# A decoder block at one token on one core: activations become the stationary matmul operand, weights and values stream 512 columns at a time

## The chip, the cores and the metric

The kernel runs on one core of a Trainium2 chip. The metric is the time of the program on the device in microseconds (us), the median of several runs. PE is TensorE (matmuls; PEld is its weight load), DVE is VectorE, ACT is ScalarE, POOL is GpSimd, and SP is SyncE, whose queue issues the big loads.

## What is computed

Eight sequences (B = 8) decode one token each through one block with D = 1024. The reference, cut to what matters:

```python
mod = (silu(c) @ w_mod).reshape(8, 6, 1, -1)            # sa, ca, ga, sb, cb, gb
h = layernorm(x) * (1 + ca) + sa
q = h @ wq                                              # 32 heads of 128
scores = q . k_cache * 128 ** -0.5                      # 4 kv heads, 8192 keys each
o = softmax(scores) @ v_cache
x = x + ga * (o @ wo)
h = layernorm(x) * (1 + cb) + sb
gate, up = h @ W_gate, h @ W_up                         # F = 3584
x = x + gb * ((gate * (gate > 0) * up) @ W_down)
```

All inputs are bf16. Eight query heads share one kv head, so there are 32 pairs (kv head, sequence), numbered n, each with 2 MB of k and 2 MB of v. With the weights 185.6 MB come from HBM, each byte once.

## The kernel before

**Recording and waits.** The program is written once, in order, through helpers (`mm`, `tr`, `dve`, `act`, `pool`). A small graph keeps each engine's instructions in that order and adds semaphore waits where one engine uses what another wrote. A PSUM bank (2 KB a partition, 8 banks) counts as one object: PE and another engine that touch the same bank wait for each other. Since all work passes through the helpers, most rows of the profile carry the helpers' lines: L278 is `mm`, L282 `tr`, L286 `dve`, L289 `act`, L510 the loads.

**Loads.** One ring of 11 x 8192 columns in SBUF takes all weights, k and v in a fixed order (`stream`): four blocks of `w_mod`, four of `wq`, then k(n) and, two pairs later, v(n), with a `wo` block for each kv head among them, then `gate` and `up` alternating, then `wd` (W_down). SP issues one DMA for each block in that order. A block that reuses ring space first waits for PE's last use of the blocks that lay there (`behind`, `users`).

**Matmuls with the weights stationary.** For mod, wq, wo, gate and up, a 128x128 piece of the weight is loaded into PE as the stationary operand, and the activations (128x8) move. The results lie transposed, output features on partitions, which is the form the next stage needs. Only `wd` works the other way: `hmT` (128x8) is stationary, 256 columns of weight move, and each of four matmuls writes another group of output partitions (0, 32, 64, 96).

**Attention.** The loop over n has eight slots j, each for 1024 keys. For a slot the kernel transposes eight 128x128 pieces of k on PE (`slot_transpose`), evicts them from PSUM (`slot_evac`: even slots DVE, odd slots ACT), multiplies the slot of two before with q (`slot_scores`, 8 matmuls), and does the values of pair n-2 (`slot_pv`, 8 matmuls with v stationary and `pt`, the exponentials, moving). Softmax of pair n-1 is spread over slots 2 to 7: `soft_max` (DVE maximum, `mp`), `soft_max_t` (transpose on PE), `soft_diag` (DVE: `nm`, then the diagonal `dg`), `soft_bc` (an f32 matmul that spreads the maximum), `soft_sub` (DVE, `ssub`), `soft_exp` (ACT, `pt`), `soft_sum` (eight matmuls with ones). `o_evac` divides by the sum at slot 0 of pair n+3. `wo_part` and `wo_add` follow every eight pairs.

**End.** After attention come the second layernorm, gate/up, relu and product (`hmT`), `wd`, and four small stores.

Of the kernel before, what the change touches and what calls it, by code (L numbers as in the profile page):

```python
# [124 lines left out]
def bass_adaLN_cond__gqa_block_cached__glu_gated_reglu__decode_kernel(  # L125
# [35 lines left out]
    with ExitStack() as es:  # L161
# [13 lines left out]
        onesb = sb("onesb", [128, 128], bf16)  # L175
# [5 lines left out]
        yacc = sb("yacc", [128, KD * B], f32)  # L181
# [13 lines left out]
        rl = sb("rl", [128, REP], f32)  # L195
        ot = sb("ot", [128, G, REP, B], bf16)
        gr = sb("gr", [128, KF * B], f32)
# [4 lines left out]
        crow, xrow, sig = (KT[0:B, i, :] for i in range(3))  # L202
        fR = ssub[:, 0:256]
# [9 lines left out]
        O = lambda i: PS[:, 5 + i, :]  # L213
        X = PS[:, 7, :]
        pS = [("ps", 0), ("ps", 1)]
        pT = [("ps", 2), ("ps", 3), ("ps", 4)]
        pO = [("ps", 5), ("ps", 6)]
        pX = ("ps", 7)
        g.psum(*pS, *pT, *pO, pX)
# [24 lines left out]
        wd_parts = [(0, 7), (7, 14), (14, 21), (21, 26), (26, 28)]  # L244
        for i, (a, z) in enumerate(wd_parts):
            block(("wd", i), (z - a) * D, B_W_down.rearrange("(p k) n -> p k n", k=KF)[:, a:z, :], (z - a, D))
# [51 lines left out]
        for t, v, k in ((identb, 0.0, "identb"), (identf, 0.0, "identf"), (onesD, 1.0 / D, "onesD"), (ones1, 1.0, "ones1"), (onesb, 1.0, "onesb")):  # L298
            pool(lambda e, t=t, v=v: e.memset(t[:], v), writes=[k])
        for t, k in ((identb, "identb"), (identf, "identf")):  # L300
            pool(lambda e, t=t: e.affine_select(out=t[:], in_=t[:], compare_op=ALU.not_equal, fill=1.0, base=0,
                                                pattern=[[-1, 128]], channel_multiplier=1), reads=[k], writes=[k])

# [7 lines left out]
        for k in range(KD):  # L311
            tr(TB(0)[:, B * k:B * (k + 1)], sig[:, k::KD], identb[0:B, 0:B], [("KT", 2), "identb"], [pT[0]])
        dve("tensor_copy", siluT[:], TB(0)[:, 0:KD * B].rearrange("p (k b) -> p k b", b=B), reads=[pT[0]], writes=["siluT"])
# [23 lines left out]
        NM = 6 * KD  # L337
        for k in range(KD):
            w = place[("mod", k // 2)][:, k % 2, :]
            for f in range(NM):  # L340
                mm(S(0)[:, B * f:B * (f + 1)], w[:, 128 * f:128 * (f + 1)], siluT[:, k, :], k == 0 and f == 0, k == KD - 1,
                   ["siluT"], [pS[0]], ("mod", k // 2))
        dve("tensor_copy", modT[:].rearrange("p s k b -> p (s k b)"), S(0)[:, 0:NM * B], reads=[pS[0]], writes=["modT"])
# [5 lines left out]
        for k in range(KD):  # L349
            w = place[("wq", k // 2)][:, k % 2, :]  # L350
            for h in range(Hq):
                mm(S(1)[:, B * h:B * (h + 1)], w[:, 128 * h:128 * (h + 1)], hT[:, k, :], k == 0 and h == 0, k == KD - 1,
                   ["hT"], [pS[1]], ("wq", k // 2))
        act(qT[:], S(1)[:, 0:Hq * B].rearrange("p (h b) -> p b h", b=B), ACT.Copy, reads=[pS[1]], writes=["qT"])
# [33 lines left out]
        def slot_pv(n, j):  # L388
            o = O(n % 2)[:, 0:REP]
            for i in range(8):  # L390
                cc = 8 * j + i
                mm(o, place[("v", n)][:, cc, :], pt[:, n % 2, REP * cc:REP * (cc + 1)], cc == 0, cc == NC - 1,
                   [("pt", n % 2)], [pO[n % 2]], ("v", n))
# [21 lines left out]

        def soft_sum(n):
            for i in range(8):
                mm(O(n % 2)[:, 64:128], onesb[:], pt[:, n % 2, 64 * i:64 * (i + 1)], i == 0, i == 7, ["onesb", ("pt", n % 2)], [pO[n % 2]])

        def o_evac(n):  # L420
            gg, b = n // B, n % B
            dve("tensor_reduce", lsum[:], O(n % 2)[:, 64:128].rearrange("p (c r) -> p r c", r=REP), AX.X, ALU.add, reads=[pO[n % 2]], writes=["lsum"])
            dve("reciprocal", rl[:], lsum[:], reads=["lsum"], writes=["rl"])
            dve("tensor_tensor", out=ot[:, gg, :, b], in0=O(n % 2)[:, 0:REP], in1=rl[:], op=ALU.mult, reads=[pO[n % 2], "rl"], writes=[("ot", gg)])

        def wo_part(gg, bank, h0, h1):
            w = place[("wo", gg)]
            for h in range(h0, h1):
                for k in range(KD):
                    mm(O(bank)[:, 128 + B * k:128 + B * (k + 1)], w[:, h, 128 * k:128 * (k + 1)], ot[:, gg, h, :], h == 0 and k == 0, h == REP - 1,  # L430
                       [("ot", gg)], [pO[bank]], ("wo", gg))

        def wo_add(gg, bank):
            y = O(bank)[:, 128:128 + KD * B]
            if gg == 0:
                dve("tensor_copy", yacc[:], y, reads=[pO[bank]], writes=["yacc"])
            else:
                dve("tensor_tensor", out=yacc[:], in0=y, in1=yacc[:], op=ALU.add, reads=[pO[bank], "yacc"], writes=["yacc"])

        for n in range(N + 4):  # L440
# [3 lines left out]
            wbank = (n - 1) % 2  # L444
            for j in range(8):
# [5 lines left out]
                if 0 <= n - 2 < N:  # L451
                    slot_pv(n - 2, j)
                if j == 0 and 0 <= n - 3 < N:
                    o_evac(n - 3)
                if wg is not None and 2 <= j <= 5:
                    wo_part(wg, wbank, 2 * (j - 2), 2 * (j - 1))
                if wg is not None and j == 6:
                    wo_add(wg, wbank)
# [95 lines left out]
```

## Time and profile before

| | |
|---|---|
| median of 3 runs | 452.18 us (452.06 to 452.18) |
| profiled execution, its own time | 452.11 us |
| its span, first to last instruction | 450.3 us |
| mean granted PE clock | 0.799 |
| PE, DVE, ACT busy | 357.0, 175.2, 155.1 us |
| read from HBM | 185.63 MB, 412 GB/s over the span |

An entry of the profile such as `L278 PE MATMUL PS<-qT,KT` reads line, engine, operation, output from inputs; `128x8 bf16 x2048` are partitions by elements, type and count. A matmul's time in a row is its passage through the pipeline; successive matmuls overlap, so the cost of a group is read from start to start in the timeline. A matmul with f32 operands appears as two. "Granted clock" is the share of PE's full clock that the throttle let through; 0.50 and 1.0 are the values recorded. "DMA share" is the mean busy share of the core's 16 DMA engines.

### The profile page before, as it was taken

To read this page: it belongs to the slowest core of one execution; us is meant where nothing else is said; L and a number is where in the kernel's file an instruction comes from. 1 tells how busy PE (TensorE), PEld (TensorE's weight loads), DVE (VectorE), ACT (ScalarE), POOL (GpSimd) and SP (SyncE) were. 2 spreads that over 40 slices of the span, in tenths; PEclk is the share of its full clock that TensorE was granted. 3 is DMA by queue.
4 is the path that set the end of the run, shared out by engine and by line. 5 is a ranking of instruction groups with operands and counts; after the bars stand their busy time and mean duration, and the time that the engine had idled before them with its cause. 6 is when DMAs were issued, how large, how long until landed. Compare 5 with 4: busy or idle time off the path is not lost.

```text
span 450.3 us, 16982 instructions
## 1 busy us (share of the span) xinstructions
PE 357.0 (79%) x8008; PEld 342.8 (76%) x8008; DVE 175.2 (39%) x422; ACT 155.1 (34%) x169; POOL 1.5 (0%) x11
## 2 busy tenths in 40 slices
PE   1525477887898959998989798898999999759973
PEld 1425377887888959888888798888889988649961
DVE  1001044554454434555544436445454446530000
ACT  3000055455444433444454335444453455400000
POOL 1000000000000000000000000000000000000000
PEclk9999998899796775888886859669787689955555
DMA  8999999999999999999999999999999999999992
GB/s 352 421 426 427 437 424 431 426 426 428 427 429 425 414 436 426 432 424 429 425 418 430 426 427 429 425 427 426 417 428 429 428 429 418 385 424 425 430 385 115
DMA packets 18101, 186.73 MB, mean 415 GB/s; under 512 B 1472, under 2 KB 1504, under 8 KB 7792
## 3 DMA queue, kind: packets, MB, share of 16 engines
q1 hardware_dynamic: 17968, 185.61, 97.6%
q8 instruction: 62, 1.02, 0.8%
q14 instruction: 7, 0.06, 0.0%
q10 hardware_dynamic: 64, 0.04, 0.0%
HBM read 185.63 MB, written 0.02 MB: 412 GB/s over the span
## 4 chain that ended last, share of the span: by engine, by line
DMA 49%; PE 35%; DVE 8%; SPq 4%; issue 3%; ACT 0%; DVEq 0%
DMA ring<-in_A_k_cache_dram 34%; PE PS L282 20%; PE PS L278 15%; DMA ring<-in_A_wq_dram 8%; DMA ring<-in_B_W_down_dram 7%; SPq L510 4%; DVE KT L286 3%; DVE mp L286 2%; DVE dg L286 1%; DVE nm L286 1%; DVE ssub L286 0%; ACT KT L289 0%; ACT pt L289 0%; DVE x1T L286 0%; DVE outR L286 0%
## 5 line engine op out<-in xcount | busy, mean ns | idle before, releaser
L282 PE MATMUL PS<-identb,ring 128*128 128x128 bf16 x2048 | 191.6, 249 | 10.9 <-DMA ring<-in_A_k_cache_dram 10.2
L289 ACT ACTIVATE KT<-PS 128x1024 bf16<-128x1024 bf16 x128 | 131.1, 1024 | 185.2 <-PE PS L282 142.9
L282 PEld LDWEIGHTS PS<-identb,ring 128*128 128x128 bf16 x2048 | 147.1, 112 | 13.7 <-DMA ring<-in_A_k_cache_dram 11.6
L286 DVE COPY KT<-PS 128x1024 bf16<-128x1024 bf16 x128 | 88.5, 692 | 149.1 <-PE PS L282 149.1
L278 PE MATMUL PS<-qT,KT 128*128 128x8 bf16 x2048 | 92.7, 169 | 0.1
L278 PE MATMUL PS<-pt,ring 128*128 128x8 bf16 x2048 | 87.3, 167 | 0.7 <-issue 0.7
L278 PEld LDWEIGHTS PS<-qT,KT 128*128 128x128 bf16 x2048 | 87.0, 102 | 0.2 <-ACT KT L289 0.2
L278 PEld LDWEIGHTS PS<-pt,ring 128*128 128x128 bf16 x2048 | 70.6, 98 | 1.0 <-issue 1.0
L278 PE MATMUL PS<-dg,ones 8*128 8x8 f32 x64 | 13.3, 278 | 25.5 <-DVE dg L286 25.5
L278 PEld LDWEIGHTS PS<-dg,ones 8*128 8x128 f32 x64 | 10.6, 204 | 28.2 <-DVE dg L286 27.8
L278 PEld LDWEIGHTS PS<-h2T,ring 128*128 128x128 bf16 x448 | 28.5, 172 | 2.0 <-DMA ring<-in_B_W_up_dram 1.6
L278 PE MATMUL PS<-h2T,ring 128*128 128x8 bf16 x448 | 28.7, 204 | 1.5 <-DMA ring<-in_B_W_up_dram 1.5
L286 DVE TENSOR_TENSOR ssub<-PS,nb 128x512 f32<-128x512 f32 x32 | 22.1, 692 | 1.2
L278 PE MATMUL PS<-siluT,ring 128*128 128x8 bf16 x384 | 10.9, 168 | 14.0 <-DMA ring<-in_w_mod_dram 14.0
L286 DVE TENSOR_REDUCE mp<-PS 128x8 f32<-128x512 f32 x32 | 21.8, 681 | 0.4 <-PE PS L278 0.4
L278 PEld LDWEIGHTS PS<-siluT,ring 128*128 128x128 bf16 x384 | 10.8, 105 | 14.3 <-DMA ring<-in_w_mod_dram 14.3
L289 ACT ACTIVATE pt<-ssub 128x512 bf16<-128x512 f32 x32 | 19.9, 622 | 3.7 <-DVE ssub L286 3.7
L278 PE MATMUL PS<-pt,onesb 128*128 128x64 bf16 x256 | 15.7, 215 | 2.6 <-ACT pt L289 2.6
L278 PE MATMUL PS<-hT,ring 128*128 128x8 bf16 x256 | 7.5, 168 | 11.2 <-DMA ring<-in_A_wq_dram 11.2
L278 PEld LDWEIGHTS PS<-hT,ring 128*128 128x128 bf16 x256 | 7.1, 104 | 11.5 <-DMA ring<-in_A_wq_dram 11.5
L289 ACT ACTIVATE qT<-PS 128x256 bf16<-128x256 f32 x1 | 0.4, 384 | 42.7 <-PE PS L278 42.7
L278 PEld LDWEIGHTS PS<-pt,onesb 128*128 128x128 bf16 x256 | 11.9, 111 | 2.8 <-ACT pt L289 2.8
(64 smaller groups left out, 107.1 us busy)
## 6 DMA issues: line engine op xcount, KB each, us to landing
ring<-in_A_k_cache_dram SPq DMA_DIRECT2D x32, 2048.0 KB, 38.3
ring<-in_A_v_cache_dram SPq DMA_DIRECT2D x32, 2048.0 KB, 37.6
ring<-in_w_mod_dram SPq DMA_DIRECT2D x4, 3072.0 KB, 20.7
ring<-in_A_wq_dram SPq DMA_DIRECT2D x4, 2048.0 KB, 42.3
ring<-in_A_wo_dram SPq DMA_DIRECT2D x4, 2048.0 KB, 43.0
ring<-in_B_W_gate_dram SPq DMA_DIRECT2D x4, 1792.0 KB, 27.9
ring<-in_B_W_up_dram SPq DMA_DIRECT2D x4, 1792.0 KB, 26.5
ring<-in_B_W_down_dram SPq DMA_DIRECT2D x3, 1792.0 KB, 28.8
```

Of the source, the lines that this page charges most:

```text
L278: return pe(lambda e: e.matmul(out_, lhsT, rhs, start=start, stop=stop, skip_group_check=True), reads, writes, block, deps)
L282: return pe(lambda e: e.matmul(out_, in_, ident, start=True, stop=True, is_transpose=True), reads, writes, block)
L286: return g.op("dve", lambda e: getattr(e, name)(*args, **kw), reads, writes)
L289: return g.op("act", lambda e: e.activation(*args, **kw), reads, writes)
L510: o.fn = (lambda e, key=key, src=src, o=o: e.dma_start(place[key], src).then_inc(o.sem, 16))
```

## The change

Every matmul with weights or values is turned round, as `wd` was before.

- **mod, wq, wo, gate, up:** the activations (128x8) are stationary and 512 columns of weight move; four successive matmuls write four groups of output partitions (0, 32, 64, 96) of one PSUM bank. The results come out in rows, one sequence a partition, so they are evicted whole and transposed back on PE: 12 f32 transposes for mod, 8 bf16 for q, 8 bf16 for `hmT`. The banks are zeroed first by DVE memsets, since the partitions between the groups are not written. The wo results add up in rows (`yR`), and four f32 matmuls with the selector `pick` turn them at the end.
- **PV:** 32 columns of `pt` (4 key pieces x 8 heads) are stationary and 512 columns of v move, 16 matmuls a pair in slots 1, 3, 5 and 7. Of the result V, four diagonal blocks are wanted. ACT copies the bank (`pv_evac`, slot 0 of pair n+3), four f32 matmuls with the selector `sel` add the blocks into Y (`pv_pick`, slot 1), and `o_evac` is in slot 2.
- **Sum:** a DVE reduction over `pt` (`soft_part`, slot 6) and one f32 matmul with ones (`soft_sum`, slot 7) replace the eight matmuls.
- **Softmax pieces:** `soft_max` moves from slot 2 to 1 and its transpose from 3 to 2; `soft_diag` is in slot 3, `soft_bc` and `soft_sub` in 4, `soft_exp` in 5. Each PE piece now stands one slot after the DVE piece that feeds it.
- **`wd` loads:** another split of the rows of W_down, with 8 KB and 4 KB runs per partition instead of 14, 10 and 4 KB. All other loads, their order and their ring places stay.

The diff, cut:

```diff
...
+        wd_parts = [(0, 2, 0, 4), (2, 4, 0, 4), (4, 6, 0, 4), (6, 7, 0, 2), (6, 7, 2, 4)]
+        for i, (a, z, i0, i1) in enumerate(wd_parts):
+            block(("wd", i), (z - a) * (i1 - i0) * D, B_W_down.rearrange("(c p i) n -> p c (i n)", p=128, i=4)[:, a:z, D * i0:D * i1],
+                  (z - a, (i1 - i0) * D))
...
+        dve("tensor_reduce", sel[:], identf[:].rearrange("p (q x) -> p x q", q=4), AX.X, ALU.add, reads=["identf"], writes=["sel"])
+        dve("tensor_reduce", pick[:], identf[:].rearrange("p (s h x) -> p h x s", s=2, h=2)[:, :, 0:B, :], AX.X, ALU.add, reads=["identf"], writes=["pick"])
+        for bank, key in ((S(0), pS[0]), (S(1), pS[1]), (T(0), pT[0]), (Y, pY)):
+            dve("memset", bank, 0.0, writes=[key])
...
-        NM = 6 * KD
+        mbank = [(S(0), pS[0]), (S(1), pS[1]), (T(0), pT[0])]
         for k in range(KD):
             w = place[("mod", k // 2)][:, k % 2, :]
-            for f in range(NM):
-                mm(S(0)[:, B * f:B * (f + 1)], w[:, 128 * f:128 * (f + 1)], siluT[:, k, :], k == 0 and f == 0, k == KD - 1,
-                   ["siluT"], [pS[0]], ("mod", k // 2))
-        dve("tensor_copy", modT[:].rearrange("p s k b -> p (s k b)"), S(0)[:, 0:NM * B], reads=[pS[0]], writes=["modT"])
+            for f in range(12):
+                j, q = f // 4, f % 4
+                mm(mbank[j][0][32 * q:32 * q + B, :], siluT[:, k, :], w[:, 512 * f:512 * (f + 1)], k == 0, k == KD - 1,
+                   ["siluT"], [mbank[j][1]], ("mod", k // 2))
+        for j in range(3):
+            if j == 1:
+                act(modR[j], mbank[j][0], ACT.Copy, reads=[mbank[j][1]], writes=[("KT", j)])
+            else:
+                dve("tensor_copy", modR[j], mbank[j][0], reads=[mbank[j][1]], writes=[("KT", j)])
+        tbank = [(T(1), pT[1]), (T(2), pT[2]), (V, pV)]
+        for j in range(3):
+            t, key = tbank[j]
+            for i in range(4):
+                tr(t[:, 128 * i:128 * (i + 1)], modR[j][:, 128 * i:128 * (i + 1)], identf[:], [("KT", j), "identf"], [key])
+            dve("tensor_copy", modT[:].rearrange("p s k b -> p (s k) b")[:, 16 * j:16 * (j + 1), :].rearrange("p (q i) b -> p i q b", i=4),
+                t.rearrange("p (i q x) -> p i q x", i=4, q=4)[:, :, :, 0:B], reads=[key], writes=["modT"])
...
-            for h in range(Hq):
-                mm(S(1)[:, B * h:B * (h + 1)], w[:, 128 * h:128 * (h + 1)], hT[:, k, :], k == 0 and h == 0, k == KD - 1,
-                   ["hT"], [pS[1]], ("wq", k // 2))
-        act(qT[:], S(1)[:, 0:Hq * B].rearrange("p (h b) -> p b h", b=B), ACT.Copy, reads=[pS[1]], writes=["qT"])
+            for f in range(8):
+                j, q = f // 4, f % 4
+                mm(S(j)[32 * q:32 * q + B, :], hT[:, k, :], w[:, 512 * f:512 * (f + 1)], k == 0, k == KD - 1,
+                   ["hT"], [pS[j]], ("wq", k // 2))
...
-        def slot_pv(n, j):
-            o = O(n % 2)[:, 0:REP]
-            for i in range(8):
-                cc = 8 * j + i
-                mm(o, place[("v", n)][:, cc, :], pt[:, n % 2, REP * cc:REP * (cc + 1)], cc == 0, cc == NC - 1,
-                   [("pt", n % 2)], [pO[n % 2]], ("v", n))
+
+        def pv(n, t):
+            for q in range(4):
+                cc = 16 * t + 4 * q
+                mm(V[32 * q:32 * (q + 1), :], pt[:, n % 2, REP * cc:REP * (cc + 4)],
+                   place[("v", n)][:, cc:cc + 4, :].rearrange("p c d -> p (c d)"), t == 0, t == 3, [("pt", n % 2)], [pV], ("v", n))
+
+        def pv_evac(n):
+            act(ov[:], V, ACT.Copy, reads=[pV], writes=["ov"])
+
+        def pv_pick(n):
+            for i in range(4):
+                mm(Y[:, 0:REP], ov[:, 128 * i:128 * (i + 1)], sel[:, REP * i:REP * (i + 1)], i == 0, i == 3, ["ov", "sel"], [pY])
...
+        def soft_part(n):
+            dve("tensor_reduce", lsum[:], pt[:, n % 2, :].rearrange("p (c r) -> p r c", r=REP), AX.X, ALU.add, reads=[("pt", n % 2)], writes=["lsum"])
+
         def soft_sum(n):
-            for i in range(8):
-                mm(O(n % 2)[:, 64:128], onesb[:], pt[:, n % 2, 64 * i:64 * (i + 1)], i == 0, i == 7, ["onesb", ("pt", n % 2)], [pO[n % 2]])
+            mm(X[:, 136:136 + REP], onesf[:], lsum[:], True, True, ["onesf", "lsum"], [pX])
+            dve("reciprocal", rl[:, n % 2, :], X[:, 136:136 + REP], reads=[pX], writes=[("rl", n % 2)])
 
         def o_evac(n):
             gg, b = n // B, n % B
-            dve("tensor_reduce", lsum[:], O(n % 2)[:, 64:128].rearrange("p (c r) -> p r c", r=REP), AX.X, ALU.add, reads=[pO[n % 2]], writes=["lsum"])
-            dve("reciprocal", rl[:], lsum[:], reads=["lsum"], writes=["rl"])
-            dve("tensor_tensor", out=ot[:, gg, :, b], in0=O(n % 2)[:, 0:REP], in1=rl[:], op=ALU.mult, reads=[pO[n % 2], "rl"], writes=[("ot", gg)])
-
-        def wo_part(gg, bank, h0, h1):
+            dve("tensor_tensor", out=ot[:, gg, :, b], in0=Y[:, 0:REP], in1=rl[:, n % 2, :], op=ALU.mult, reads=[pY, ("rl", n % 2)], writes=[("ot", gg)])
+
+
+        def wo_part(gg, h0, h1):
             w = place[("wo", gg)]
             for h in range(h0, h1):
-                for k in range(KD):
-                    mm(O(bank)[:, 128 + B * k:128 + B * (k + 1)], w[:, h, 128 * k:128 * (k + 1)], ot[:, gg, h, :], h == 0 and k == 0, h == REP - 1,
-                       [("ot", gg)], [pO[bank]], ("wo", gg))
-
-        def wo_add(gg, bank):
-            y = O(bank)[:, 128:128 + KD * B]
+                for half in range(2):
+                    a = 64 * (h % 2) + 32 * half
+                    mm(Y[a:a + B, :], ot[:, gg, h, :], w[:, h, 512 * half:512 * (half + 1)], h < 2, h >= REP - 2, [("ot", gg)], [pY], ("wo", gg))
+
+        def wo_add(gg):
             if gg == 0:
-                dve("tensor_copy", yacc[:], y, reads=[pO[bank]], writes=["yacc"])
+                dve("tensor_copy", yR[:], Y, reads=[pY], writes=["yR"])
             else:
-                dve("tensor_tensor", out=yacc[:], in0=y, in1=yacc[:], op=ALU.add, reads=[pO[bank], "yacc"], writes=["yacc"])
+                dve("tensor_tensor", out=yR[:], in0=Y, in1=yR[:], op=ALU.add, reads=[pY, "yR"], writes=["yR"])
 
         for n in range(N + 4):
             wg = (n - 11) // B if n >= 11 and (n - 11) % B == 0 else None
             if n == N + 3:
                 wg = G - 1
-            wbank = (n - 1) % 2
             for j in range(8):
                 if n < N:
                     slot_transpose(n, j)
                     slot_evac(n, j)
                 if 0 <= 8 * n + j - 2 < 8 * N:
                     slot_scores(8 * n + j - 2)
-                if 0 <= n - 2 < N:
-                    slot_pv(n - 2, j)
-                if j == 0 and 0 <= n - 3 < N:
-                    o_evac(n - 3)
-                if wg is not None and 2 <= j <= 5:
-                    wo_part(wg, wbank, 2 * (j - 2), 2 * (j - 1))
+                if 0 <= n - 3 < N:
+                    if j == 0:
+                        pv_evac(n - 3)
+                    elif j == 1:
+                        pv_pick(n - 3)
+                    elif j == 2:
+                        o_evac(n - 3)
+                if 0 <= n - 2 < N and j % 2 == 1:
+                    pv(n - 2, j // 2)
+                if wg is not None and 3 <= j <= 6:
+                    wo_part(wg, 2 * (j - 3), 2 * (j - 2))
                 if wg is not None and j == 6:
-                    wo_add(wg, wbank)
+                    wo_add(wg)
                 if 0 <= n - 1 < N:
-                    if j == 2:
+                    if j == 1:
                         soft_max(n - 1)
+                    elif j == 2:
+                        soft_max_t(n - 1)
                     elif j == 3:
-                        soft_max_t(n - 1)
+                        soft_diag(n - 1)
                     elif j == 4:
-                        soft_diag(n - 1)
                         soft_bc(n - 1)
+                        soft_sub(n - 1)
                     elif j == 5:
-                        soft_sub(n - 1)
+                        soft_exp(n - 1)
                     elif j == 6:
-                        soft_exp(n - 1)
+                        soft_part(n - 1)
                     elif j == 7:
                         soft_sum(n - 1)
...
-        dve("tensor_tensor", out=x1T[:].rearrange("p k b -> p (k b)"), in0=yacc[:], in1=modT[:, 2].rearrange("p k b -> p (k b)"), op=ALU.mult, reads=["yacc", "modT"], writes=["x1T"])
+        for i in range(4):
+            mm(X[:, 16 * i:16 * (i + 1)], yR[:, 128 * i:128 * (i + 1)], pick[:].rearrange("p h b -> p (h b)"), True, True, ["yR", "pick"], [pX])
+        dve("tensor_tensor", out=x1T[:].rearrange("p (h i) b -> p h i b", h=2), in0=X[:, 0:64].rearrange("p (i h b) -> p h i b", i=4, h=2),
+            in1=modT[:, 2].rearrange("p (h i) b -> p h i b", h=2), op=ALU.mult, reads=[pX, "modT"], writes=["x1T"])
...
+        for j in range(2):
+            dve("memset", S(j), 0.0, writes=[pS[j]])
+            dve("memset", T(j), 0.0, writes=[pT[j]])
+        dve("memset", V, 0.0, writes=[pV])
         for k in range(KD):
-            for half, nm_ in ((0, "gate"), (1, "up")):
+            for bank, keys, nm_ in ((S, pS, "gate"), (T, pT, "up")):
                 w = place[(nm_, k // 2)][:, k % 2, :]
-                for f in range(KF):
-                    mm(S(half)[:, B * f:B * (f + 1)], w[:, f::KF], h2T[:, k, :], k == 0 and f == 0, k == KD - 1,
-                       ["h2T"], [pS[half]], (nm_, k // 2))
-        act(gr[:], S(0)[:, 0:KF * B], ACT.Relu, reads=[pS[0]], writes=["gr"])
-        dve("memset", PS[:, 2, 0:256], 0.0, writes=[pT[0]])
-        dve("tensor_tensor", out=hmT[:].rearrange("p k b -> p (k b)"), in0=S(1)[:, 0:KF * B], in1=gr[:], op=ALU.mult, reads=[pS[1], "gr"], writes=["hmT"])
-
-
-        for i, (a, z) in enumerate(wd_parts):
-            for k in range(a, z):
-                for q in range(4):
-                    mm(PS[32 * q:32 * q + B, 2, 0:256], hmT[:, k, :], place[("wd", i)][:, k - a, 256 * q:256 * (q + 1)], k == 0, k == KF - 1,
-                       ["hmT"], [pT[0]], ("wd", i))
-        dve("tensor_tensor", out=fR, in0=PS[:, 2, 0:256], in1=gbR[:], op=ALU.mult, reads=[pT[0], "gbR"], writes=["ssub"])
+                for f in range(7):
+                    j, q = f // 4, f % 4
+                    mm(bank(j)[32 * q:32 * q + B, :], h2T[:, k, :], w[:, 512 * f:512 * (f + 1)], k == 0, k == KD - 1,
+                       ["h2T"], [keys[j]], (nm_, k // 2))
+        for j in range(2):
+            act(gr[j], S(j), ACT.Relu, reads=[pS[j]], writes=[("KT", j)])
+            dve("tensor_tensor", out=hmR[:, 512 * j:512 * (j + 1)], in0=T(j), in1=gr[j], op=ALU.mult, reads=[pT[j], ("KT", j)], writes=[("KT", 2 + j)])
+
+        for j in range(2):
+            for i in range(4):
+                tr(TB(2)[:, 512 * j + 128 * i:512 * j + 128 * (i + 1)], hmR[:, 512 * j + i:512 * (j + 1):4], identb[:], [("KT", 2 + j), "identb"], [pT[2]])
+        for j in range(2):
+            nq = 4 - j
+            dve("tensor_copy", hmT[:, 16 * j:16 * j + 4 * nq, :].rearrange("p (q i) b -> p i q b", i=4),
+                TB(2)[:, 512 * j:512 * (j + 1)].rearrange("p (i q x) -> p i q x", i=4, q=4)[:, :, 0:nq, 0:B], reads=[pT[2]], writes=["hmT"])
+
+
+        for n, (a, z, i0, i1) in enumerate(wd_parts):
+            for c_ in range(a, z):
+                for i in range(i0, i1):
+                    for q in range(4):
+                        at = D * (i - i0) + 256 * q
+                        mm(V[32 * q:32 * q + B, 0:256], hmT[:, 4 * c_ + i, :], place[("wd", n)][:, c_ - a, at:at + 256], c_ + i == 0, c_ == 6 and i == 3,
+                           ["hmT"], [pV], ("wd", n))
...
```

## The prediction

> **What bounds the kernel now.** I read the page first, then the stages, then the waits, then single instructions.
>
> ```profile
> PE 357.0 (79%) x8008; PEld 342.8 (76%) x8008; DVE 175.2 (39%) x422; ACT 155.1 (34%) x169; POOL 1.5 (0%) x11
> ...
> DMA  8999999999999999999999999999999999999992
> ...
> q1 hardware_dynamic: 17968, 185.61, 97.6%
> q8 instruction: 62, 1.02, 0.8%
> ```
>
> TensorE (PE) is busiest of the compute engines, but the DMA engines stand at 9 from slice 2 to 39, and q1 fills 97.6% of 16 engines' span. The chain of waits (DMA 49%, PE 35%) misleads about PE: during PE's pieces of it the loads ran on.
>
> The stages show what the last slice hides (last columns: granted clock, DMA share, GB/s):
>
> ```profile
> 60.00:390.00 330.00, 289.75 (x6564) 282.29 (x6562) 162.26 (x376) 148.36 (x160) 0.00 (x0) 0.81 1.01 425
> 400.00:430.00 30.00, 25.59 (x393) 24.76 (x393) 2.92 (x12) 0.21 (x1) 0.00 (x0) 0.50 1.02 427
> 437.00:445.00 8.00, 3.45 (x60) 1.60 (x56) 0.00 (x0) 0.00 (x0) 0.00 (x0) 0.50 0.49 204
> 446.40:450.30 3.90, 0.57 (x8) 0.08 (x8) 0.85 (x2) 0.00 (x0) 0.00 (x0) 0.50 0.02 4
> ```
>
> From 437 to 445 us half of the DMA capacity idles while PE waits for `wd` blocks: some engines are done and others are not. The trace keeps the 16 increments by which each load reports. Their spread, first to last, is 0.74 us for the first load, 1.7 at the load landing at 33.6, and 10.1 at 349.4. It grows in steps, at the landings of 88.6, 138.6, 198.6, 244.1, 299.0, 349.4 and 399.1: seven steps of 1.2 to 1.4 us, 1.3 on average. The packets of q8, PE's instruction fetch (16,384 B each), number 62 from 18.0 to 439.1 us; their durations repeat with period eight (934, 933, 924, 968, 960, 949, 886, 886 ns), so I read them as dealt in turn to eight engines. Packets 9, 17, 25, 33, 41, 49 and 57 start at 86.1, 136.1, 192.5, 241.8, 293.5, 345.7 and 394.8: each step belongs to one packet of the first of these engines. That engine carries 8 packets. The last load's first increment comes at 437.0 and its last at 446.33; then 3.97 us of matmuls, two DVE operations and stores end the span. So the bound is the slowest DMA engine: its share of the loads plus eight fetches.
>
> PE has little room in attention:
>
> ```profile
> PE PS L278 <- DVE dg L286: 25.5, 31, 1.4
> PE PS L282 <- DMA ring<-in_A_k_cache_dram: 10.2, 8, 3.6
> ```
>
> It waits only 10.2 us in all for k, and 25.5 us for `dg`.
>
> **The change, part by part.**
> *Fetches.* Matmuls removed: 2048 (PV) + 256 (sums) + 384 + 256 + 448 (mod, wq, gate/up) + 256 (wo) = 3648. Added: 512 + 96 + 64 + 112 + 64 for the same, 28 transposes of the row results (12 + 8 + 8), and f32 ones that count double in this trace (`dg` is x64 for 32): 128 picks (256), 32 sums (64), 4 final picks (8), together 1204. That leaves 8008 - 3648 + 1204 = 5564. Each has a weight load, so PE runs 11,128 instructions and 16 others. Before, 16,032 / 256 = 62.6 gave 62 packets; 11,144 / 256 = 43.5 gives 43. The first engine gets packets 1, 9, 17, 25, 33 and 41: 6 instead of 8. Gain 2 x 1.3 = 2.6 us (2.4 to 2.8 by the smallest and largest step).
>
> [...]
>
> *`wd` blocks.* Packets of 14,336, 10,240 and 4,096 B took 535, 385 and 159 ns; those of 8,192 B took 309. Per engine (8 partitions) 8 x (3 x 535 + 385 + 159) = 17.19 us becomes 8 x (6 x 309 + 2 x 159) = 17.38: +0.2 us. Ring places before `wd` don't change, so every k, v and wo load waits for the same release.
>
> *PE in attention.* One (k, v) pair takes the loads (388.5 - 58.0) / 32 = 10.33 us, `wo` included. PE must stay below that. Rows at full clock, then at half:
>
> ```profile
> 108.93 0.38 PE L278 MATMUL PS<-dg,ones 8*128 8x8 f32 x2 [0.84 <-DVE dg L286]
> 109.24 0.62 PE L282 MATMUL PS<-identb,ring 128*128 128x128 bf16 x8
> 109.70 0.34 PE L278 MATMUL PS<-qT,KT 128*128 128x8 bf16 x8
> 109.90 0.34 PE L278 MATMUL PS<-pt,ring 128*128 128x8 bf16 x8
> 110.11 0.61 PE L282 MATMUL PS<-identb,ring 128*128 128x128 bf16 x8
> ...
> 176.75 0.59 PE L278 MATMUL PS<-dg,ones 8*128 8x8 f32 x2 [0.39 <-DVE dg L286]
> 177.27 1.03 PE L282 MATMUL PS<-identb,ring 128*128 128x128 bf16 x8
> ...
> 437.86 1.67 PE L278 MATMUL PS<-ring,hmT 128*8 128x256 bf16 x28 [0.74 <-DMA ring<-in_B_W_down_dram]
> ```
>
> From start to start: a slot is 0.45 + 0.20 + 0.20 (transposes, scores, PV) at full clock and, by its rows around 179, 0.81 + 0.26 + 0.21 at half; an f32 pair 0.31 and 0.52. The `wd` row has the new form, four groups of output partitions: 1.67 / 28 = 60 ns for 256 columns at clock 0.50, so 119 for 512; at full clock between 60 and 119, I take 60, since rows that stream columns nearly halve. A pair after, full clock: 8 x 0.65 = 5.2; PV 16 x 0.06 = 0.95; four picks 4 x 0.31 = 1.24; sum 0.31; `dg` 0.31; max transpose 0.11; total 8.1. At half: 8 x 1.07 + 1.9 + 2.1 + 0.52 + 0.52 + 0.16 = 13.8. Before: 8.6 with its waits, and 11.7.
>
> *Waits.* One slot later, max transposes and `dg` find their inputs ready: up to 0.99 us a pair goes. New: the sum waits for a DVE reduction of `pt` (its nearest row, `mp`, 681 ns) queued behind an eviction; the next transposes stand behind it. Bounds 0 to 1.0; I take 0.5. The picks wait for ACT's copy of V (nearest row `pt`, 622 ns), covered by a slot and a half on PE; uncovered it costs 0.6. DVE rises by about 0.5 to 5.9 us a pair, ACT by 0.6 to 5.3: no bound. So 8.6 and 14.3. With before's clock (0.81, 38% of the time at half) a pair takes 1 / (0.62 / 8.6 + 0.38 / 14.3) = 10.1 us, just below 10.33. An estimate says the clock rises: at full clock every 3.41 us step with 23 or more transposes started in it was followed by full clock, and steps of 54 eight-column matmuls alone (405 to 426) always by half. Streamed columns count; PV adds 16 x 512 columns a quarter wide, as much as 16 transposes to 64.
>
> [...]
>
> *Outside attention.* mod and wq rows wait 14.0 and 11.2 us for loads; 24 matmuls a block at 0.119 (2.9 us) take what 96 took (2.75). Their evictions, transposes and copies add about 2.5 us before `qT`; scores begin some 0.5 us later, within the ring's cover. At the start two reductions and four memsets go ahead of DVE's work for `siluT`; by the 0.27 us of a 256-column memset they take about 3 us, and DVE waited 4.3 us before `siluT`. Between attention and gate/up come the last pair's picks and V copy (2.1 + 0.6), its sum's reduction (0.7), the final picks (4 x 0.52) and five memsets of 512 columns (2.7 by twice that row): 8.2 us, so gate/up starts near 413 instead of 404.7. It needs 112 x 0.119 = 13.3 us where 448 took 28.7, so it is still level with the last `up`, landing at 429.3: that delay costs nothing under this cover, and all its 8.2 us without it. If column groups didn't overlap, it would take 53 us. The new transposes of `hm` fall before `wd`, which trails the loads. Nothing after the last load changes.
>
> *Sum.* The profiled execution took 452.11 us (span 450.3 + 1.8), 0.07 below the median. 452.11 - 2.6 + 0.2 = 449.7.
>
> **Rivals.** (1) Slower: PE becomes the bound. Decisive point: 10.33 us a pair. If picks cost 0.5 each at full clock (between the 0.31 of `dg` and the 0.69 of the two-instruction `onesD` matmul), and the clock stays, a pair takes 1 / (0.62 / 9.4 + 0.38 / 14.3) = 10.8: +0.47 x 32 = 15 us, 465. For it: only 10.2 us of waiting for k now. Against: clock and waits above. (2) The lag isn't the fetches': 452.3. Against: seven steps, seven packets. (3) The slowest engine gets 5 fetches (other dealing): 448.4.
>
> **How the numbers follow.** Forecast 66% (448.6 to 450.7), rival 3 5%, rival 2 9%, rival 1 20%. No change means within 0.2% (0.9 us), about what can be told. Faster 0.71, same 0.09, slower 0.20. 448.2 to 456 leaves out most of rival 1 and a little elsewhere: under 2 in 10.
>
> **What would show it.** q8 with 43 packets; the half-share stretch shorter by about 2.6 us; waits of PE for k larger, for `dg` gone; clock above 0.81 in attention. Wrong if PE's waits for k vanish and GB/s falls below 425 there.

## The result and the profile after

The changed kernel takes 449.67 us (median of four runs, 449.48 to 449.86) against 452.18 (four runs beside it): ratio 0.9944, interval 0.9927 to 0.9961, so 2.5 us faster. The profiled execution took 449.48 us with a span of 447.5, against 452.11 and 450.3.

The page of the changed kernel, engines, DMA slices and queues:

```profile
PE 371.3 (83%) x5564; PEld 294.7 (66%) x5564; DVE 211.0 (47%) x442; ACT 172.3 (39%) x203; POOL 1.5 (0%) x11
...
DMA  8999999999999999999999999999999999999992
...
q1 hardware_dynamic: 18352, 185.61, 98.0%
q8 instruction: 43, 0.70, 0.6%
```

PE runs 30% fewer matmuls, and yet it is busy for 14 us more: fewer instructions are not less work. The DMA row has not changed. q8, the instruction fetch, has 43 packets where it had 62.

The stages (times of PE, PEld, DVE, ACT, POOL, then granted clock, DMA share, GB/s):

```profile
60.00:390.00 330.00, 309.13 (x4936) 263.68 (x4934) 185.05 (x373) 159.95 (x186) 0.00 (x0) 0.84 1.01 427
400.00:430.00 30.00, 21.86 (x190) 11.43 (x190) 7.68 (x24) 3.10 (x5) 0.00 (x0) 0.58 1.02 427
437.00:443.60 6.60, 3.42 (x64) 1.69 (x60) 0.00 (x0) 0.00 (x0) 0.00 (x0) 0.50 0.40 168
443.60:447.50 3.90, 0.54 (x8) 0.05 (x8) 0.85 (x2) 0.00 (x0) 0.00 (x0) 0.50 0.02 4
```

In attention PE went from 290 to 309 us busy in 330, at a clock of 0.84 instead of 0.81, and the loads run at 427 GB/s (425 before). At the end there is the same stretch with part of the DMA engines idle, and the same 3.9 us after it. The trace's landing records (the 16 increments by which each load reports that it has landed) say where the 2.6 us of the profiled executions came from: the last load's last increment comes at 443.50 instead of 446.33. Eight of its increments come from 434.91 to 438.2 and eight from 441.9 to 443.50; before, eight came by 438.2 and eight from 444.7 on. Read as one increment for each engine, half of the engines are far behind, as many as the fetches seem to be dealt to. (The first increment comes earlier too, 434.91 instead of 437.00; SP was done with issuing the first gate block at 380.9 instead of 383.6. But the engines in front do not set the end.) The spread between first and last increment grows in six steps of 1.2 to 1.3 us, at the landings of 33.7, 127.6, 192.5, 257.4, 327.1 and 400.6; q8's packets 1, 9, 17, 25, 33 and 41 start 2.4 to 4.9 us ahead of each. Before there were eight steps, the first of them (0.9) at 26.2.

The waits of PE, the list by line waited for (total us, times, longest):

```profile
PE PS L285 <- DVE lsum L293: 18.9, 25, 2.7
...
PE PS L289 <- DMA ring<-in_A_k_cache_dram: 3.6, 3, 2.4
...
PE PS L285 <- DVE dg L293: 0.3, 1, 0.3
```

The wait for `dg` (25.5 us before) has gone, and a wait for `lsum`, the new DVE reduction, has taken most of its place. PE's wait for k, 10.2 us before, has nearly gone too: PE no longer arrives ahead of the loads. The rows of two pairs show why, from the timeline of PE; those at 107.97 and 108.52 are at half clock, the others at full clock:

```profile
102.28 0.34 PE L285 MATMUL PS<-qT,KT 128*128 128x8 bf16 x8
102.55 0.40 PE L285 MATMUL PS<-ring,pt 128*32 128x512 bf16 x4
102.89 0.62 PE L289 MATMUL PS<-identb,ring 128*128 128x128 bf16 x8
103.34 0.34 PE L285 MATMUL PS<-qT,KT 128*128 128x8 bf16 x8
103.55 0.61 PE L289 MATMUL PS<-identb,ring 128*128 128x128 bf16 x8
103.99 0.34 PE L285 MATMUL PS<-qT,KT 128*128 128x8 bf16 x8
104.26 0.40 PE L285 MATMUL PS<-ring,pt 128*32 128x512 bf16 x4
105.27 0.39 PE L285 MATMUL PS<-lsum,onesf 128*128 128x8 f32 x2 [0.61 <-DVE lsum L293]
...
107.97 0.62 PE L285 MATMUL PS<-ring,pt 128*32 128x512 bf16 x4
108.52 1.03 PE L289 MATMUL PS<-identb,ring 128*128 128x128 bf16 x8
...
119.24 1.04 PE L285 MATMUL PS<-sel,ov 128*128 128x8 f32 x8
120.20 0.40 PE L285 MATMUL PS<-ring,pt 128*32 128x512 bf16 x4
```

From start to start, four PV matmuls take 102.89 - 102.55 = 0.34 us, 85 ns each. The scores ahead of them take 0.27 (102.28 to 102.55) where scores ahead of transposes take 0.21 (103.34 to 103.55): 0.06 to 0.07 more at each change of form, also ahead of `dg`. The sum's matmul starts 1.01 us after the last PV group, 0.67 more than that group needs. Four picks take 0.96. A pair at full clock: slots 5.2, five changes of form 0.35, PV 1.35, picks 0.96, sum 0.24, `dg` 0.32, `mp` 0.11, wait 0.67, together 9.2 us, or 9.1 if the change behind the picks is in their 0.96 already. With the half-clock rows (a PV group 0.55, picks 1.79 from 401.07 to 402.86) the 14.3 of the prediction hardly changes. At a clock of 0.84 (32% at half) that is 1 / (0.68 / 9.2 + 0.32 / 14.3) = 10.4 us, or 10.3 with 9.1, beside 10.33 for the loads.

### The profile page after: what moved, and what is told of

Its sections match the earlier page's. It is cut to its first block, busy times and chain, and to the rows that moved or that the text cites. A ratio compares the mean times of both kernels' runs of the same rounds, so it can differ in the third digit from the quotient of the medians.

```text
span 447.5 us, 12119 instructions
## 1 busy us (share of the span) xinstructions
PE 371.3 (83%) x5564; PEld 294.7 (66%) x5564; DVE 211.0 (47%) x442; ACT 172.3 (39%) x203; POOL 1.5 (0%) x11
## 4 chain that ended last, share of the span: by engine, by line
PE 58%; DMA 28%; DVE 9%; SPq 2%; ACT 1%; issue 1%
PE PS L289 30%; PE PS L285 29%; DMA ring<-in_A_k_cache_dram 11%; DMA ring<-in_A_wq_dram 11%; DMA ring<-in_B_W_down_dram 6%; DVE lsum L293 4%; DVE KT L293 3%; SPq L577 2%; ACT KT L296 0%; DVE yR L293 0%; DVE qT L293 0%; ACT pt L296 0%; DVE ssub L293 0%; ACT ov L296 0%; DVE mp L293 0%
## 5 line engine op out<-in xcount | busy, mean ns | idle before, releaser
L296 ACT ACTIVATE KT<-PS 128x1024 bf16<-128x1024 bf16 (+1 forms) x132 | 133.2, 1010 | 232.3 <-PE PS L289 152.4
L293 DVE COPY KT<-PS 128x1024 bf16<-128x1024 bf16 (+1 forms) x130 | 89.8, 691 | 146.1 <-PE PS L289 122.7
L285 PE MATMUL PS<-ring,pt 128*32 128x512 bf16 x512 | 60.3, 469 | 0.0
L285 PE MATMUL PS<-sel,ov 128*128 128x8 f32 x256 | 37.8, 275 | 0.8 <-ACT ov L296 0.7
L285 PEld LDWEIGHTS PS<-sel,ov 128*128 128x128 f32 x256 | 35.6, 214 | 1.8 <-ACT ov L296 1.8
L293 DVE TENSOR_REDUCE lsum<-pt 128x8 f32<-128x512 bf16 x32 | 34.0, 1062 | 2.4 <-ACT pt L296 2.4
L285 PE MATMUL PS<-lsum,onesf 128*128 128x8 f32 x64 | 12.7, 270 | 18.9 <-DVE lsum L293 18.9
L285 PE MATMUL PS<-ring,siluT 128*8 128x512 bf16 x96 | 10.9, 625 | 14.4 <-DMA ring<-in_w_mod_dram 14.4
L296 ACT ACTIVATE ov<-PS 128x512 f32<-128x512 f32 x32 | 18.9, 592 | 4.8 <-PE PS L285 4.8
L285 PEld LDWEIGHTS PS<-ring,pt 128*32 128x32 bf16 x512 | 13.4, 97 | 3.2 <-issue 0.5
```

The costliest lines, as they stand in the source:

```text
L285: return pe(lambda e: e.matmul(out_, lhsT, rhs, start=start, stop=stop, skip_group_check=True), reads, writes, block, deps)
L293: return g.op("dve", lambda e: getattr(e, name)(*args, **kw), reads, writes)
L296: return g.op("act", lambda e: e.activation(*args, **kw), reads, writes)
```

## The experiments

My theory after the result: the end is set by the slowest DMA engine, which carries its share of the loads and every eighth instruction fetch, so only the number of fetches on that engine counts (the trace does not name the engine of an increment or a packet; that it is one engine is read from the times); PE stands level with the loads in attention, without deciding. The rivals: the gain is spread evenly over all fetches or comes from elsewhere (PE's waits, DVE), or PE decides already.

**Fetches added alone.** In both kernels PE runs extra matmuls that nothing reads, in mod (and wq) where it waits for loads. The first adds 400:

```diff
+            for _ in range(50):
+                mm(V[:, 0:B], identb[:], siluT[:, k, :], True, True, ["siluT", "identb"], [pV])
```

> The changed kernel with 400 idle matmuls more (8 columns, 50 after each k of the mod stage, where PE waits for w_mod): 800 PE instructions, 11,944 / 256 = 46 fetch packets instead of 43. Theory 1 (the end is the slowest DMA engine; each fetch on it costs 1.3 us; packets are dealt to eight engines): the first engine still carries packets 1, 9, 17, 25, 33, 41, so 6, and the time stays at 449.7 (within 0.4). Rival A (fetches cost their share of all engines, smoothly, 1.3 / 8 each): 450.2. Rival B (the gain came from PE's path, not from fetches): 449.7, as PE has 14 us of waiting in the mod stage.

The second, 80 after each of the eight k of mod and 57 after seven of wq:

```diff
+            for _ in range(80):
+                mm(V[:, 0:B], identb[:], siluT[:, k, :], True, True, ["siluT", "identb"], [pV])
...
+            for _ in range(57 if k < KD - 1 else 0):
+                mm(V[:, 0:B], identb[:], siluT[:, k, :], True, True, ["siluT", "identb"], [pV])
```

> The changed kernel with 1,039 idle matmuls more in the mod and wq stages (80 after each k of mod, 57 after each k of wq but the last): 2,078 PE instructions, 13,222 / 256 = 51 fetch packets. Theory 1: packet 49, on the first engine, comes before 400 us, so 7 fetches instead of 6 and 449.7 + 1.3 = 451.0; the half-share stretch at the end is 1.3 us longer, and a new step of 1.3 us stands in the spread of the landings. Rival A: 8 x 0.16 = +1.3 as well, but without a step. Rival B: 449.7, since the idle matmuls (27 us) lie in PE's waits for loads (23 us) and attention doesn't change.

Measured: 449.65 us (ratio 0.9944, 0.9931 to 0.9956) and 451.01 (0.9973, 0.9962 to 0.9984). The fetch queue in the page of the one and of the other:

```profile
q8 instruction: 46, 0.75, 0.6%
```

```profile
q8 instruction: 51, 0.84, 0.7%
```

Three more packets cost nothing, eight cost 1.34 us. In the second kernel packet 49 starts at 401.0, a seventh step of 1.3 us follows at the landing of 406.3, and the last load lands at 445.12 instead of 443.50; PE still waits for it and starts its last eight matmuls at 445.16. A cost spread over all packets would have shown in the first kernel, with some 0.5 us. Without any cost the second would have stayed at 449.7.

**Less work on PE in attention.** The copy of V and the selector become bf16, so that a pick is one instruction instead of two (V is rounded to bf16 by this).

```diff
-        ov = sb("ov", [128, 512], f32)
-        sel = sb("sel", [128, 32], f32)
+        ov = sb("ov", [128, 512], bf16)
...
+        sel = sb("sel", [128, 32], bf16)
...
```

> The changed kernel with the copy of V and the selector in bf16, so that the four picks are one instruction each: 10,888 PE instructions, 42 packets; PE rid of 0.6 to 0.9 us a pair. Theory 1: packet 41 still comes in time, 6 fetches, 449.7 (within 0.4), and PE's waits for k rise from 3.6 us to 15 or more. Rival B (PE's path sets the time in attention, where it has only 3.6 us of waiting left): 1 to 10 us less.

Measured: 449.47 us (0.994, 0.9926 to 0.9953). Its waits of PE and its attention stage:

```profile
PE PS L290 <- DMA ring<-in_A_k_cache_dram: 35.2, 15, 6.8
PE PS L286 <- DVE lsum L294: 23.2, 32, 2.7
```

```profile
60.00:390.00 330.00, 271.00 (x4914) 227.89 (x4911) 190.36 (x384) 164.22 (x192) 0.00 (x0) 0.90 1.01 427
```

PE is busy for 38 us less in attention (its clock rose too, to 0.90) and spends most of that waiting for k; the loads run as before and the time stays. PE did not decide.

**More work on PE in attention.** One pick, or all four, are done twice in each pair (the repeat replaces the first).

```diff
-            for i in range(4):
+            for i in [0, 0, 1, 2, 3]:
```

> One more f32 pick in every pair (the first of the four is done twice, and its repeat replaces it). It adds 0.24 us a pair on TensorE at full clock and 0.46 at half by the changed kernel's rows, about 0.3 x 32 = 10 us over attention; q8 44 packets, still six on the first engine in time. Theory A (the DMA engines set the end, TensorE is just level with the loads in attention and gate/up has some margin behind them): TensorE's few waits for k vanish, attention ends up to 8 us later, and some 0 to 4 us of that shows: 449.6 to 454. Theory B (TensorE has room in attention, the clock rises with the work): 449.5, and waits for k remain.

```diff
-            for i in range(4):
+            for i in [0, 1, 2, 3, 0, 1, 2, 3]:
```

> Every f32 pick twice: 0.96 us a pair more at full clock, 1.84 at half, about 1.2 x 32 = 38 us over attention, 45 packets of q8. Theory A: TensorE now sets the pace, a pair takes about 11.4 instead of 10.33 us, the loads wait for ring space and GB/s falls to about 390: 470 to 487. Theory B: under 455.

With one pick more: 449.63 us (0.9941, 0.9924 to 0.9957). PE's list of waits has no entry for k any more. Gate/up starts at 422.06 instead of 419.49, so PE fell 2.6 us further behind, and none of it reached the end:

```profile
422.06 0.60 PE L285 MATMUL PS<-ring,h2T 128*8 128x512 bf16 x4 [1.26 <-DVE PS L293]
...
436.43 1.67 PE L285 MATMUL PS<-ring,hmT 128*8 128x256 bf16 x32 [1.36 <-DMA ring<-in_B_W_down_dram]
```

With four more the four executions took 493.57 to 520.12 us (median 512.99), more than the 470 to 487 expected. The trace is of the fastest, and I read only the rough size from it. From 260 to 430 us:

```profile
260.00:430.00 170.00, 165.21 (x2292) 141.02 (x2288) 82.06 (x167) 69.19 (x82) 0.00 (x0) 0.74 0.88 355
```

Now the DMA engines wait (0.88, 355 GB/s), as they would if the ring comes free too late. So the point from which PE decides lies, by the rows' times, between 0.3 and 1.2 us a pair above the changed kernel, and past it the loss is steep: 32 x 1.2 = 38 us were added, 44 and more came out, with a clock of 0.76, 0.81 and 0.74 in the stretches 60 to 160, 160 to 260 and 260 to 430 (0.83 and 0.88 in the first two in the changed kernel). Whether the extra f32 matmuls lower the clock was not tried by itself.

**The slots of before.** Only the loop's slot assignments of the softmax pieces go back (`soft_max` in slot 2, its transpose in 3, and so on).

```diff
-                    if j == 1:
+                    if j == 2:
                         soft_max(n - 1)
-                    elif j == 2:
+                    elif j == 3:
                         soft_max_t(n - 1)
-                    elif j == 3:
+                    elif j == 4:
                         soft_diag(n - 1)
...
```

> The changed kernel with the softmax pieces in the slots they had before (maximum in slot 2, its transpose 3, diagonal and spread 4, subtraction 5, exponential 6, sum 7). 43 packets as in the changed kernel. Theory 1 with PE at its limit in attention: PE waits only 3.6 us for k in the changed kernel, so what the moved slots save (0.15 + 0.84 us a pair before, and the wait for the sum grows by up to 1 us) comes back in full: 1 to 2 us x 32 = 32 to 64 us above 449.7, less what a higher clock share gives back; 475 to 510. If the loads still cover it: 449.7, with no wait of PE for k left.

Measured: 487.01 us (1.0763, 1.0731 to 1.0795). Waits of PE, and the GB/s by slice:

```profile
PE PS L285 <- DVE dg L293: 31.9, 32, 1.0
...
PE PS L285 <- DVE lsum L293: 12.9, 19, 1.8
...
PE PS L289 <- DVE mp L293: 5.8, 19, 0.5
```

```profile
GB/s 358 420 426 429 434 428 429 429 429 431 430 427 422 428 431 424 403 431 428 416 427 379 378 292 314 428 410 352 386 354 359 285 320 400 422 351 313 427 259 3
```

One microsecond a pair of waits for `dg` is back. Before the change PE had room for such a wait (25.5 us in all); with the longer pair it has not. The loads keep some 427 GB/s until half-way and then fall. I read that as the time PE takes to use up what the ring holds ahead.

**Attention alone, and all but attention.** The first kernel turns only PV, sum, wo and the slots; mod, wq, gate/up and W_down are those of before. The second is its complement. Both edits are shown against the changed kernel.

```diff
-                for f in range(7):
-                    j, q = f // 4, f % 4
-                    mm(bank(j)[32 * q:32 * q + B, :], h2T[:, k, :], w[:, 512 * f:512 * (f + 1)], k == 0, k == KD - 1,
...
+                for f in range(KF):
+                    mm(S(half)[:, B * f:B * (f + 1)], w[:, f::KF], h2T[:, k, :], k == 0 and f == 0, k == KD - 1,
...
```

> Only attention and wo turned round (PV, sum, picks, wo, softmax slots of the changed kernel); mod, wq, gate/up and W_down as before. 6,352 matmuls, 12,720 PE instructions, 49 fetch packets. Theory 1: packets 1 to 41 of the first engine count, packet 49 comes near 429 us, ahead of the last loads, so 7 fetches: 452.1 - 1.3 = 450.8 (449.5 if packet 49 is too late). If the gain came from attention's PE work alone: 449.7.

```diff
-        def pv(n, t):
-            for q in range(4):
...
+        def slot_pv(n, j):
+            o = O(n % 2)[:, 0:REP]
...
```

> Only mod, wq, gate/up and W_down turned round; attention and wo as before. 7,220 matmuls, 14,456 PE instructions, 56 fetch packets, packet 49 near 350 us: 7 fetches on the first engine. Theory 1: 452.1 - 1.3 + 0.2 = 451.0. If the gain came from attention alone: 452.3.

All but attention: 451.14 us (0.9977, 0.9968 to 0.9986), with 56 packets, seven on the slow engine: as expected.

```profile
q8 instruction: 56, 0.92, 0.7%
```

Attention alone: 454.79 (1.0037, 1.0007 to 1.0066), between 450.69 and 456.69. That I had not expected. Of its 49 packets the last starts at 443.0, too late for a step, and with six fetches the last load lands at 443.68. The timeline of PE at its end:

```profile
415.38 28.54 PE L283 MATMUL PS<-h2T,ring 128*128 128x8 bf16 x448
444.50 5.71 PE L283 MATMUL PS<-ring,hmT 128*8 128x256 bf16 x112 [0.57 <-DVE hmT L291]
```

Gate/up with stationary weights took 28.54 us, and it started 10.7 us later than before the change (404.69); W_down's matmuls then came after all loads instead of beside them. Two more kernels undo one half each, to tell gate/up from mod and wq: the change without mod and wq, and the change without gate, up and W_down (the edit above).

```diff
-                mm(mbank[j][0][32 * q:32 * q + B, :], siluT[:, k, :], w[:, 512 * f:512 * (f + 1)], k == 0, k == KD - 1,
...
+            for f in range(NM):
+                mm(S(0)[:, B * f:B * (f + 1)], w[:, 128 * f:128 * (f + 1)], siluT[:, k, :], k == 0 and f == 0, k == KD - 1,
...
```

> The whole change except mod and wq, which keep their weights stationary as before. TensorE runs 12,064 instructions: 47 packets of q8, packets 1, 9, 17, 25, 33 and 41 on the first engine, no 49th. Theory A (the end is the slowest DMA engine with six fetches; what made the attention-only version late was the gate and up stage with weights stationary): 449.5, within 0.4. Theory B (the attention-only version was late because mod and wq were left as they were and attention began or ran worse for it): 451 to 455, scattered.

> The whole change except gate, up and the split and order of W_down, which are as before. TensorE runs 11,800 instructions: 46 packets, six on the first engine. Theory A: the longer end of attention has lost its cover: gate/up starts near 417 (419.5 less the five memsets), takes 28.5 us, so W_down's matmuls start near 446 and take 5.7 us, and the time is 455 to 457 although the last load has landed near 443.6. Theory B: 450, because those 28 us had slack as they had before the change.

Without mod and wq: 449.45 us (0.9938, 0.9921 to 0.9954), 47 packets, the same time as the whole change. Without gate, up and W_down: 457.42 (1.0087, 1.0052 to 1.0122), 451.59 to 458.12. Its timeline:

```profile
418.02 28.54 PE L284 MATMUL PS<-h2T,ring 128*128 128x8 bf16 x448
447.13 5.78 PE L284 MATMUL PS<-ring,hmT 128*8 128x256 bf16 x112 [0.57 <-DVE hmT L292]
```

Its last load landed at 443.38, and W_down's matmuls began only at 447.13. So the turned attention needs the turned gate/up, and mod and wq are neutral here. The wide scatter of both kernels fits an end that follows PE's pace through attention; that is argued, since the trace holds one execution.

**The uneven DMA engines.** Two attempts to use the engines that finish early. The last 1 MB of W_down goes in 16 DMAs of eight partitions (the trace of the change has one packet for each partition's run: 256 packets of 4,096 B for the two W_down blocks of 512 KB), first from SP:

```diff
-        wd_parts = [(0, 2, 0, 4), (2, 4, 0, 4), (4, 6, 0, 4), (6, 7, 0, 2), (6, 7, 2, 4)]
+        wd_parts = [(0, 2, 0, 4), (2, 4, 0, 4), (4, 6, 0, 4), (6, 7, 0, 4)]
...
+            for p in range(0, 128, 8):
+                ins = e.dma_start(place[key][p:p + 8], src[p:p + 8]).then_inc(sem, 16)
```

> The changed kernel with the last 1 MB of W_down loaded as 16 DMAs of 8 partitions instead of two of 128. A DMA of 8 rows can occupy 8 engines at most, so if it is always the same eight these take 4.9 us for it instead of 2.4, and the other eight nothing. Theory 1: if they are the eight that carry no fetches, the slowest engine is rid of 2.4 us and the time falls to 447.3; if they are the fetching ones, it rises to 452.1. If no engine is behind at the end (lag theory wrong): 452.1 too, but then the landings' spread is small before it.

then from GpSimd's queue, each behind a tiny DMA of eight rows, meant to shift it by eight engines:

```diff
+                e.dma_start(junk[:, 4 * i:4 * i + 4], c[:, 4 * i:4 * i + 4]).then_inc(tsem, 16)
+                ins = e.dma_start(place[key][8 * i:8 * i + 8], src[8 * i:8 * i + 8]).then_inc(wsem, 16)
```

> As in the run with the last 1 MB of W_down in 16 DMAs of 8 partitions, but issued from GpSimd's queue, each behind a DMA of 8 rows of 8 bytes. That run showed the eight engines used by SP to be those with the fetches. If this queue deals each DMA to the next eight engines in turn, the tiny ones fall on the fetching eight and the large ones on the others: 447.3 (2.4 us less than 449.7). If it uses the same eight: 452 to 456. Issue costs of GpSimd are unknown here.

Measured: 455.29 us (1.007, 1.0057 to 1.0083) and 467.48 (1.0336, 1.0316 to 1.0355); neither hit its expectation. In the first, the whole load before the split one has its first increment at 432.37 as in the changed kernel, but its last at 444.64 instead of 441.05, and the last of all comes at 448.27. So the short DMAs took the engines that were late already, for which 452.1 was expected. The time is about 3 us above that; why was not followed up. In the second, GB/s by slice:

```profile
GB/s 342 436 423 427 436 427 429 427 432 427 427 428 416 433 427 428 431 427 431 424 421 434 425 427 425 434 425 422 428 429 429 427 414 425 399 257 244 267 337 20
```

While the packets of GpSimd's DMAs ran (405 to 442 us), all loads together fell to some 250 GB/s. Whether the queue, the eight-partition shape or the tiny DMAs did that was not tried. The 8.6 us between the first and the last engine stay unused.

## Why the prediction was right, and where it was not

**Right: the bound and the fetches.** The sum gave 449.7; the profiled execution took 449.48 and the median is 449.67, by the mechanism named. The kernels whose loads set the end, without the two that split the last load, by fetches on the slow engine:

| fetches on it | kernels (packets of q8) | us |
|---|---|---|
| 6 | bf16 picks (42), the change (43), one pick more (44), 400 idle matmuls (46), mod and wq as before (47) | 449.45 to 449.67 |
| 7 | 1,039 idle matmuls (51), all but attention (56) | 451.01, 451.14 |
| 8 | before (62) | 452.18 |

The time goes in steps, by 1.3 to 1.7 and 1.0 to 1.2 us, and not with the number of packets between the steps. (The kernel before has the other split of W_down's loads, which counts for 0.1.) Nor is any version here faster than the changed kernel by more than the intervals allow. One packet for each full 256 PE instructions fits the counts (62 for 16,032, 43 for 11,144, 51 for 13,222, 56 for 14,456). In these runs a fetch cost its time through the loads: with a seventh on the slow engine the last load landed at 445.12 instead of 443.50, and PE's last matmuls waited for it. A packet's own record lasts 0.88 to 0.97 us and the step is 1.2 to 1.3 before and after the change (the first one before, 0.9; 0.9 to 1.7 in the traces of the others); where the difference comes from is open.

**Right: `wd`, the tail and the wait for `dg`.** Nothing changed after the last load; `dg`'s wait went. The last load came 2.83 us earlier instead of 2.4, and the profiled time is 2.63 less: the last `up` block landed 2.93 earlier (426.41 instead of 429.34), and W_down's blocks took 17.09 us instead of 16.99 from there, +0.1 and not +0.2. Two steps of 1.2 to 1.33 make at most 2.7 of the 2.93; the rest is not accounted for.

**Wrong: the room of PE.** Forecast were larger waits for k; they fell from 10.2 to 3.6 us. The terms that failed are sizes in the pair of 8.6 us, which measured 9.1 to 9.2:
- PV was taken at the lower end, 60 ns a matmul, and took 85; the change of form, 0.07 us up to five times a pair, was not in the sum.
- The wait for the sum was taken at 0.5 and is 0.67 in the rows above. The reduction was priced by `mp`, 681 ns; over `pt` it takes longer (bf16, read with a stride; which of the two costs the time was not tried):

```profile
L293 DVE TENSOR_REDUCE lsum<-pt 128x8 f32<-128x512 bf16 x32 | 34.0, 1062 | 2.4 <-ACT pt L296 2.4
L293 DVE TENSOR_REDUCE mp<-PS 128x8 f32<-128x512 f32 x32 | 22.1, 692 | 4.9 <-PE PS L285 0.8
```

- The picks were cheaper than said, 0.96 instead of 1.24.

So the pair stood at 10.3 to 10.4 us, on the decisive point of the first rival, where the prediction had 10.1. That the forecast time held in spite of this was partly luck, and it has a reason that the prediction gave only in part. At the level of 10.33 us PE only falls behind slowly, the ring holds some of it, and gate/up covers what is left at the end: one pick more pushed it 2.6 us later at no cost. The prediction's test for this rival (waits for k vanish and GB/s falls) named two things that need not come together: with one pick more the first happened without the second (427 GB/s from 60 to 390 us); with four more, both.

**Wrong in size, harmless: the start of gate/up.** PE's last transposes of k and first rows of gate/up, before and after:

```profile
387.48 0.61 PE L282 MATMUL PS<-identb,ring 128*128 128x128 bf16 x8
...
404.69 23.22 PE L278 MATMUL PS<-h2T,ring 128*128 128x8 bf16 x364
```

```profile
392.61 1.01 PE L289 MATMUL PS<-identb,ring 128*128 128x128 bf16 x8
...
419.49 0.59 PE L285 MATMUL PS<-ring,h2T 128*8 128x512 bf16 x4 [1.25 <-DVE PS L293]
420.47 9.05 PE L285 MATMUL PS<-ring,h2T 128*8 128x512 bf16 x108 [0.39 <-DVE PS L293]
```

Forecast 413, measured 419.49, 14.8 us later than before instead of 8.2. The last transposes of k start 5.1 us later than before (392.61 against 387.48), which is PE's lag; the time between them and gate/up grew by the remaining 9.7, where the prediction had 8.2. The cover held: 112 matmuls took 10 us and W_down's waited for loads. Where gate/up was left as before the cover was missing, and the price came out as 7.8 us (457.42 against 449.67). That it is near the prediction's 8.2 is partly chance: gate/up began 13.3 us later than before the change (418.02 against 404.69), and some of that was slack.

**Right in direction: the clock.** 0.84 in attention, from 0.81. That streamed columns count was the prediction's estimate, and gate/up fits it: before the change PE was busy without a break with matmuls of 8 columns (405.7 to 415.9 us) and the clock stayed at 0.50; after it PE was busy without a break with matmuls of 512 columns from 421.5 to 428.4, and the clock was 0.50 up to 424.9 and 0.99 in the rest. In attention PV streams 16 x 512 columns a pair, as many columns as the 64 transposes of 128 do. How much they weigh no run shows, and what raised the clock there was not tried by itself.

## What to carry to other kernels

Where loads fill all DMA engines, look at when each of their increments lands, not at the mean share: here the slowest engine set the end (8.6 us behind the first), and it was one that, by the times, also carried instruction fetches. So TensorE instructions cost time here in steps of some 8 x 256 (1.34 us from 43 to 51 packets), even those that only filled PE's waits in mod and wq, as long as their packet came early enough to delay the last load (packet 49 did at 401.0 us, and not at 443.0). A change that lengthens a stage with room may be free on its own and still spend the cover of the next one; undo the parts singly to see which part pays and which part only protects. Work out the room of the second-busiest engine per period, with both clocks, since past that point each microsecond a pair counted 32 times and more here (38 us added, 44 and more came out).

## What the runs showed of the hardware that was not expected

- DMAs of eight partitions from SP went, by the times, to the engines that were behind by the fetches: the load before them ended 3.6 us later on its last engine (444.64 instead of 441.05) and no later on its first (432.37).
- While 1 MB in eight-partition DMAs, each behind a tiny one, ran from GpSimd's queue, the total went down from 427 to about 250 GB/s.
- A matmul of another form (32 stationary columns, or eight rows) after full 128x128 ones started 0.06 to 0.07 us late (0.27 instead of 0.21 from start to start); four 512-column matmuls on four groups of output partitions took 0.34 us at full clock and 0.55 at half.
